# A hand-ordered attention-and-MLP kernel: the first loads cut into smaller pieces and moved between two DMA queues, and every step placed in a new order

## The chip, the cores and the metric

The kernel runs on one core of one Trainium2 chip. The core has five engines that run their own instruction streams: PE (TensorE, matrix products; its weight loads are listed apart as PEld), DVE (VectorE), ACT (ScalarE), POOL (GpSimd) and SP (SyncE, which here only issues DMA transfers). DMA transfers are issued from two queues: SP's, and ACT's, where the issuing instruction stands between ACT's arithmetic. The metric is device microseconds of one execution, lower is better.

## The reference

One normalised input feeds two branches, and the results are added to the input (2048 tokens of 448 features, 16 heads of 28, 1792 hidden features):

```
xn = layernorm(x)
q, k, v = split(xn @ wqkv)                       # 16 heads of 28
pq, pk = q @ w_phi, k @ w_phi                    # per head
phi = concat(softmax(p), softmax(-p))            # for q and for k
kv  = phi_k^T v ;  z = sum over tokens of phi_k
A   = (phi_q kv / (phi_q z + 1e-6)) @ wo
h   = xn @ w1 + b1 ;  act = h * tanh(softplus(h))   # "mish"
out = x + A + act @ w2
```

The matrix `w_phi` is folded into the query and key weights in the kernel: `Wpq = Wq w_phi` and `Wpk = Wk w_phi` are computed once, on PE.

## The kernel before

The 2048 tokens are 16 tiles of 128 (t = 0 to 15), taken in 8 pairs u. 448 features are three chunks of 128 rows and a tail of 64; a product over a chunk of 64 rows uses one half of PE's rows, so two products of a pair of tiles run side by side (the profile's rows of form `64*128`), and each pair's product is cut into the parts A, B (six matmuls each) and H (two, for the tail).

Nothing is scheduled by a compiler. A table of names, `ORDER` (line 147), lists about 600 steps; each step is a small function that appends instructions to the engines' streams, and every engine executes its own stream strictly in the order of the table. Waits between engines are derived from the data. PSUM has 8 banks, used as four pairs; a step takes the pair that was used least recently at that place in the table (`take2`, line 421), so the table also decides which earlier read must be over before a product may start.

The names that matter here (a digit is the tile, the pair or the chunk; a letter at the end is the engine: a ACT, d DVE, p POOL, s SP's queue, b both ACT and DVE, m DMA):

- `lxA.B` loads x tiles A to B-1; `lkm`, `lkt` load the main rows and the tail rows of Wk (`lkt` brings the tail of Wk and Wv for one half of the rows, 64x896), `lvm`, `lvt` the main rows of Wv and the other tail (64x448); `lqT0-3` load Wq transposed, a DMA transpose each (`load_qT`, L307); `lp` loads w_phi in 4 transfers, `lb` b1; `l1c0-2`, `l1t` W1 by chunks of rows and its tail, `l2p0-3` W2 in four parts, `lo` Wo.
- `st` statistics of a tile, `rt`/`rs` its 1/std, `xn` the normalised tile, `xt` its transpose (by PE and a read-out, or by DMA when it ends in m).
- `wtk0`, `wtk1` transpose the two halves of Wk on PE (L583); `wmk`, `wmq` compute Wpk and Wpq (L613). `wtk1` needs the tail that `lkt` brings.
- `v`, `k`, `q` are the three projections of a pair (L464); the read-out of k and q is two exponentials on ACT (L720, L793), that of v a copy on ACT or DVE (L544, L546).
- `kn`, `kc` turn the exponentials of k into softmax values: a sum and a reciprocal on DVE (L728 to L741), two multiplications on POOL (L732, L744). `kn` does one sign, `kc` both.
- `kv` (L761) sums phi_k^T v over all pairs; `kvz` reads it out; `e` transposes the q exponentials by DMA (L801); `nd` (L834) computes numerator and denominator of a tile; `ot` transposes the result by DMA; `wo` (L956) multiplies by Wo.
- `f0.n`, `f1.n` are the first MLP product of 128 hidden features over half of the tokens (L464) with mish on ACT (L814); `g` (L939) is the second; `sto`, `stt` store pairs and tiles.
- `z`, `y` are products of zeros on PE (L405) that touch no result. `qd` (L311) copies the last 64 columns of the transposed Wq, and `wmq` waits for it. `pw`, `pp`, `pv`, `pk`, `pi` set constants on POOL.

The program has three stages. In the front the loads arrive, the first four tiles are normalised and Wpk and Wpq are made. In the second stage PE runs the projections, with ACT's exponentials and POOL's multiplications behind it, up to `kv`. The last stage is the MLP and the attention output, with little else than PE's products.

Of the kernel before, what the change touches and what calls it, by code (L numbers as in the profile page):

```python
# [144 lines left out]


ORDER = """
zero pw pp table lx0.2a lkma lx2.4s lkta lvta lbs st2d st1d lx4.6a pi st3a z11 st0d lps rt1a lvms rt3a rt2p xn1a xn2d
rt0p xn3d lx10.12s b1 xn0d wtk0b wtk1b xt1a lx8.10a xt0d lqT3 wmk0a st4d lqT2 st5d wmk1a v1Ba rt4p lqT1 xn4p lqT0 v0Ba
l1c0a v1Aa lx6.8s lx12.14s l1c1s v0Ha st10d v1Ha rt5p qd v0Aa st11d k1A k1H wmq1a st9d rt10p rt9p wmq0a rt11p k0B k1B  # L150
xn5d st8d k0A rt8p st7d xn10d q0A st12d xn11d xn8p xt2m k0H st6d st13d q0H xn9d q1B lx14.16s rs3p xn7d q0B xn6d q1A
rt12p st15d rt13p k2A xn12d xt5m k2H xn13d v2Ad q1H k2B q2B st14d xt4m v2Bd q2A k5A xt3m v2Hd rs7p xt6m q2H xn15p k5B
v5Ba k5H v4Aa v5Ha v4Ha xn14a kn2.0 k4H kn0.0 kc5 kn2.1 k4A v4Ba v5Aa k4B e2 k3B e3 xt7m v6Hd l1c2s v6Ad k3H q4H k3A
l1ts v6Bd e0 q4B kn0.1 k6B kn4.1 kn4.0 q4A pv k6H v7Bd k7H k6A k7B v7Hd los f0.8B v7Ad ep k7A f0.8H f0.6B f0.4B e5
f0.6A f0.8A f0.6H v3Ba f0.4A e8 v3Ha f0.7B v3Aa f0.1A kn1.0 f0.4H f0.7A f0.7H kc6 kn7.1 e1 f0.1H kn7.0 f0.3B f0.1B q7B
f0.3H kn1.1 f0.3A q5H kn3.1 e4 q3B q5B q3H e9 q3A q5A f1.4B kn3.0 q7H q7A f1.4A l2p1s kv0 kv7 e11 kv4 kv6 kv5 pk kv2
kv3 kv1 e14 f1.12B kvz f1.3B e10 f1.12A f1.4H wob f1.3A f1.3H f0.12B f1.12H f1.9A f1.9H f0.5H f0.5A f1.9B f0.0H f0.5B
f0.0B nd1 f0.0A f0.9A e15 f0.12H f0.9H f0.12A nd0 f0.10A e6 f0.9B f1.10B f0.10H f1.6A f1.6H nd2 l2p0a f0.10B f1.6B
l2p3s ot0m f1.10A f1.10H f1.1H f1.11B f1.1A f1.11H nd4 f1.1B f1.7B f1.11A e7 f1.8H nd3 f1.7A f1.8B f1.0H f1.0A ot1m
f1.7H f0.13H f0.13A f1.0B f1.5H f0.13B f1.8A f1.5B nd6 f0.2B f1.5A f0.2H f1.2H f0.2A f1.2A nd5 f1.13H f1.2B f1.13B  # L160
f0.11A l2p2a f0.11H nd7 q6A f1.13A q6H f0.11B ot2m q6B wo0H ot3m wo0A nd11 nd10 wo0B e12 g1 g7 e13 ot5m g0 wo3A nd12
nd13 wo2A wo2H wo3B ot6m wo2B nd14 wo3H g6 g5 g11 g4 g10 nd15 wo5B wo6A ot7m nd9 wo5A sto2 wo5H nd8 wo6B g12 g2 g8 g3
g14 ot4m wo1H wo4B wo1B wo7B wo4A wo1A wo6H wo4H wo7H wo7A sto0 g13 g9 sto1 stt14 g15 sto6 sto5 y0.1 sto3 sto4 y3.4
stt15
"""


# [942 lines left out]
```

## Time and profile before

| what | us |
|---|---|
| median of 3 runs | 155.65 |
| the three runs | 150.18, 155.79, 155.65 |
| the profiled execution's own time | 150.82 |
| its span (first to last instruction) | 149.0 |
| busy in the span: PE, DVE, ACT, POOL | 145.1, 99.3, 76.3, 43.2 |

The span is 1.82 us shorter than the time of the same execution. PE's busy time counts a matmul until its modelled end, so neighbours overlap; how fast PE really goes is read from the starts. The granted TensorE clock is 1.00 in the whole profiled execution.

```profile
PE   7897999999999999999999999999999999999996
DVE  0885999999999303089794799588993399301722
ACT  3895999998988995774757839400000000000000
POOL 5425683999999992000000000000000000000000
DMA  4999459999997038974702133943030023220252
```

Each digit is a fortieth of the span, 3.7 us, in tenths. ACT and POOL end at about half of the span, DMA is full in the first 45 us, and PE has digits under 9 in the first four slices and in the last.

### The profile page before, as it was taken

The page shows a single profiled execution, that of the slowest core. Times are in us where ns is not written, and L with a number is a line of the kernel's source. Part 1 is how long each engine was busy: PE and PEld are TensorE (multiplying, and loading weights), DVE is VectorE, ACT ScalarE, POOL GpSimd, SP SyncE. Part 2 cuts the span into 40 slices and gives each one's busy share as a digit, 9 for nine tenths or more (in the row PEclk, how much of TensorE's full clock was granted, in tenths as well). Part 3 has the DMA queues.
Part 4 walks back from the last instruction along what each step waited for, and adds up shares of the span by engine and source line. Part 5 has one row for each costly group of instructions (what it writes and reads, how often), then busy time and mean ns, then how long its engine had stood idle before and what let it go on. Part 6 is the DMA issues. An engine that isn't in the chain of part 4 may idle for free.

```text
span 149.0 us, 3632 instructions
## 1 busy us (share of the span) xinstructions
PE 145.1 (97%) x1544; PEld 75.2 (50%) x1545; DVE 99.3 (67%) x222; ACT 76.3 (51%) x91; POOL 43.2 (29%) x66
## 2 busy tenths in 40 slices
PE   7897999999999999999999999999999999999996
PEld 2464544555444484454444545545555555547453
DVE  0885999999999303089794799588993399301722
ACT  3895999998988995774757839400000000000000
POOL 5425683999999992000000000000000000000000
DMA  4999459999997038974702133943030023220252
GB/s 121 320 249 317 106 132 164 157 239 218 212 224 183 4 57 107 191 168 122 133 4 40 26 92 66 109 93 62 7 62 0 0 41 87 56 67 4 92 185 92
DMA packets 40372, 17.17 MB, mean 115 GB/s; under 512 B 34084, under 2 KB 39844, under 8 KB 40356
## 3 DMA queue, kind: packets, MB, share of 16 engines
q1 hardware_dynamic: 38148, 14.37, 48.4%
q10 hardware_dynamic: 2208, 2.56, 5.8%
q8 instruction: 12, 0.20, 0.6%
q14 instruction: 4, 0.03, 0.1%
HBM read 6.97 MB, written 1.84 MB: 59 GB/s over the span
## 4 chain that ended last, share of the span: by engine, by line
PE 90%; SPq 5%; DMA 3%; issue 0%; DVE 0%
PE PS L464 48%; PE PS L939 28%; PE PS L956 7%; DMA WqT<-in_A_wqkv_dram 3%; SPq L307 2%; PE PS L834 2%; PE PS L761 2%; SPq L330 1%; PE PS L405 1%; PE PS L613 1%; SPq L287 1%; SPq L334 0%; SPq L290 0%; PE PS L921 0%; DVE WqT L311 0%
## 5 line engine op out<-in xcount | busy, mean ns | idle before, releaser
L464 PE MATMUL PS<-xnT,W 64*128 64x512 bf16 x392 | 45.3, 376 | 0.0
L939 PE MATMUL PS<-W,actT 128*128 128x448 bf16 (+1 forms) x224 | 42.7, 351 | 0.0
L814 ACT ACTIVATE actT<-PS,b1T 128x1024 bf16<-128x1024 f32 x28 | 30.1, 1112 | 12.2 <-PE PS L464 12.2
L939 PEld LDWEIGHTS PS<-W,actT 128*128 128x128 bf16 x224 | 21.6, 98 | 20.7 <-issue 1.3
L464 PEld LDWEIGHTS PS<-xnT,W 64*128 64x128 bf16 x392 | 18.1, 94 | 21.3 <-ACT actT L814 0.8
L904 DVE TENSOR_TENSOR x_all<-PS,x_all 128x448 bf16<-128x448 f32 (+1 forms) x16 | 9.3, 615 | 17.0 <-PE PS L956 9.2
L732 POOL TENSOR_TENSOR actT<-actT,rSk 128x896 bf16<-128x896 bf16 x12 | 20.0, 1697 | 0.0
L720 ACT ACTIVATE actT<-PS 128x896 bf16<-128x896 f32 x16 | 14.2, 1034 | 0.7 <-PE PS L464 0.7
L464 PE MATMUL PS<-Wpk,xnT 64*128 64x448 bf16 x112 | 13.2, 349 | 0.0
L464 PE MATMUL PS<-Wkv,xnT 64*128 64x448 bf16 x112 | 13.1, 349 | 0.1
L464 PE MATMUL PS<-Wpq,xnT 64*128 64x448 bf16 x112 | 13.0, 349 | 0.0
L728 DVE TENSOR_REDUCE Sk<-actT 128x32 f32<-128x896 bf16 x12 | 12.5, 1040 | 0.0
L849 DVE COPY Sq<-PS 128x16 f32<-128x16 f32 x32 | 4.0, 168 | 12.1 <-PE PS L834 12.1
L501 DVE BATCH_NORM_STATS2 stats<-x_all 128x6 f32<-128x448 bf16 x15 | 9.2, 610 | 4.1 <-DMA x_all<-in_A_x_dram 4.1
L860 DVE TENSOR_TENSOR xn<-v_all,rden 128x448 bf16<-128x448 f32 x16 | 10.0, 624 | 2.2 <-DMA Wkv<-xn 1.7
L857 DVE TENSOR_TENSOR v_all<-v_all 128x464 f32<-128x464 f32 x16 | 10.3, 643 | 0.6
L853 DVE TENSOR_TENSOR v_all<-PS,Sq 128x464 f32<-128x464 f32 x16 | 10.3, 641 | 0.5
L855 DVE TENSOR_TENSOR v_all<-PS,Sq 128x464 f32<-128x464 f32 x16 | 10.1, 630 | 0.0
L793 ACT ACTIVATE actT<-PS 128x896 bf16<-128x896 f32 x10 | 8.8, 987 | 0.3 <-PE PS L464 0.3
L464 PEld LDWEIGHTS PS<-Wkv,xnT 64*128 64x128 bf16 x112 | 5.3, 94 | 5.5 <-ACT actT L720 0.3
L464 PEld LDWEIGHTS PS<-Wpq,xnT 64*128 64x128 bf16 x112 | 5.3, 94 | 5.3 <-ACT Eq L793 0.3
L464 PEld LDWEIGHTS PS<-Wpk,xnT 64*128 64x128 bf16 x112 | 5.4, 94 | 5.1 <-ACT actT L793 0.4
(84 smaller groups left out, 135.5 us busy)
## 6 DMA issues: line engine op xcount, KB each, us to landing
out_dram<-x_all SPq DMA_DIRECT2D x7, 224.0 KB, 2.2
W<-in_B_w_dram SPq DMA_DIRECT2D x3, 448.0 KB, 4.9
x_all<-in_A_x_dram SPq DMA_DIRECT2D x5, 224.0 KB, 4.4
W<-in_B_w_dram ACTq DMA_DIRECT2D x2, 448.0 KB, 3.8
x_all<-in_A_x_dram ACTq DMA_DIRECT2D x3, 224.0 KB, 3.8
Wo<-in_A_wo_dram SPq DMA_DIRECT2D x2, 336.0 KB, 5.3
W<-in_B_w_dram SPq DMA_DIRECT2D x2, 224.0 KB, 4.9
Wkv<-in_A_wqkv_dram ACTq DMA_DIRECT2D x1, 336.0 KB, 4.4
```

What stands on the lines that cost most here:

```text
L464: ins = e.matmul(o, lhs(c, k), rhs(c, k), start=first and n == at[par][0], stop=last and n == at[par][-1])
L720: op("ACT", lambda e, s=s: e.activation(E_of(u)[:, s, :, :], two(b, D), ACT.Exp, scale=1.0 if s == 0 else -1.0), r=[pb(b), pb(b + 1)], w=[ ...
L728: op("DVE", lambda e: e.tensor_reduce(Sk[u][:, s, :], Eh(), AX.X, ALU.add), r=[("E", u, s)], w=[("Sk", u, s)], tag=f"Sk{u}.{s}")
L732: op("POOL", lambda e: e.tensor_tensor(Eh(), Eh(), ap_on(rSk[u][:, s, 0:1], [[1, 2 * H], [0, DH]]), ALU.mult), r=[("E", u, s), ("rSk", u, ...
L814: op("ACT", lambda e: e.activation(actT[:, q, fc, :], bank(b, 2), ACT.Mish, bias=b1T[:, fc:fc + 1]), r=[("b1T",), pb(b), pb(b + 1)], w=[(" ...
L853: op("DVE", lambda e: e.tensor_tensor(tv(t1[i]), num(0), sx(1), ALU.mult), r=[pb(b), pb(b + 1), ("Sq", i, 1)], w=[("t1", i)], tag=f"ta{t}")
L855: op("DVE", lambda e: e.tensor_tensor(tv(t2), num(1), sx(0), ALU.mult), r=[pb(b), pb(b + 1), ("Sq", i, 0)], w=[("t2",)], tag=f"tb{t}")
L857: op("DVE", lambda e: e.tensor_tensor(t1[i], t1[i], t2, ALU.add), r=[("t1", i), ("t2",)], w=[("t1", i)], tag=f"tc{t}")
L860: op("DVE", lambda e: e.tensor_tensor(o_sb[(t // 2) % 2][:, t % 2, :].rearrange("p (h d) -> p h d", d=DH), t1[i][:, :, 0:DH], ap_on(rden[i ...
L904: op("DVE", lambda e: e.tensor_tensor(x_all[:, t, 0:n], bank(b)[:, 0:n], x_all[:, t, 0:n], ALU.add), r=[pb(b), ("x", t)], w=[("out", t)], ...
L939: ins = e.matmul(bank(b)[:, 0:width(t)], act_of(fc, t), W2[:, fc, 0:width(t)], start=first and fc == 0, stop=last and fc == FC - 1)
L956: ins = e.matmul(bank(b)[:, 0:w], oT_of(u)[lo:hi, cc * P:(cc + 1) * P], Wo[lo:hi, cc, 0:w], start=first and n == at[par][0], stop=last and ...
```

## The change

Only `ORDER` is different: not one function, tile or instruction form is new, but the same steps stand in another order, and some in another variant (another queue or engine). The first six lines of the table before and after:

```diff
-zero pw pp table lx0.2a lkma lx2.4s lkta lvta lbs st2d st1d lx4.6a pi st3a z11 st0d lps rt1a lvms rt3a rt2p xn1a xn2d
-rt0p xn3d lx10.12s b1 xn0d wtk0b wtk1b xt1a lx8.10a xt0d lqT3 wmk0a st4d lqT2 st5d wmk1a v1Ba rt4p lqT1 xn4p lqT0 v0Ba
-l1c0a v1Aa lx6.8s lx12.14s l1c1s v0Ha st10d v1Ha rt5p qd v0Aa st11d k1A k1H wmq1a st9d rt10p rt9p wmq0a rt11p k0B k1B
...
+lx1.2s zero lx2.4a lx0.1a st1d lbs table st2d lkms pw pi st3a lkta lps lx4.6s rt1p st0d xn1d rt2a z7 y2.4 lx8.12s lvma
+xn2d rt0a b1 lqT3 rt3p xn0d xn3d wtk0a lqT2 wtk1d lvta xt0b st5d xt1a st4d wmk0a lqT1 wmk1a v0Ba v1Aa st8d lqT0 v0Aa
+rt4a rt8p rt5p st11d st10d rs5p qd v1Ha lx6.8s v0Ha k1H st9d lx12.14s v1Ba xn5d lx14.16s l1ts k1B k0H xn4d wmq0a l2p3s
```

The x tiles 0 and 1 come one by one from two queues, tiles 8 to 11 in one transfer from SP's queue. `lkm` goes from ACT's queue to SP's, `lvm` the other way. On ACT's queue `lkt`, `lvm` and `lvt` now stand between ACT's first statistics and read-outs; the load of x tiles 8 and 9 and of W1's first piece, which stood behind them, are gone from there. W1's pieces come after the query weights: the tail first, chunk 0 on SP's queue behind the first DMA transpose of x, chunks 1 and 2 on ACT's queue between the exponentials. The line numbers of the changed kernel are one less, since the table is one line shorter.

ACT's stream from its start, before: all weight loads but Wv's main rows and Wq stand ahead of the arithmetic.

```order
L351 ACT_TABLE_LOAD
L287 DMA x_all<-in_A_x_dram 128x896
L290 DMA Wkv<-in_A_wqkv_dram 128x3x448
L304 DMA Wkv<-in_A_wqkv_dram 64x896
L304 DMA Wkv<-in_A_wqkv_dram 64x448
L287 DMA x_all<-in_A_x_dram 128x896
L493 ACTIVATE junk,mv<-x_all 128x448
```

ACT's stream from its start, after (`L492` to `L496` are the statistics of tile 3, `L512`, `L514` the 1/std of tiles 2 and 0, `Eq` and `xnT` the read-outs of `wtk0` and of the transposed x):

```order
L286 DMA x_all<-in_A_x_dram 128x896
L286 DMA x_all<-in_A_x_dram 128x448
L350 ACT_TABLE_LOAD
L492 ACTIVATE junk,mv<-x_all 128x448
L494 ACTIVATE rmean<-mv 128x1
L496 ACTIVATE junk,mv<-x_all,rmean 128x448
L303 DMA Wkv<-in_A_wqkv_dram 64x896
L512 ACTIVATE lnv<-mv,eps_col 128x1
L514 ACTIVATE rstd<-lnv 128x1
L289 DMA Wkv<-in_A_wqkv_dram 128x3x448
```

Three loads that stood at the head of the streams are now issued only when ACT has reached the statistics of tile 3 and the 1/std of tile 2; `wtk1` needs the first of them, and `L494` and `L496` wait for the results of the rows before them.

SP's stream up to the first transposes of x, before and after:

```order
L287 DMA x_all<-in_A_x_dram 128x896
L334 DMA b_rows<-in_B_b_dram 14x128
L330 DMA Wbd<-in_A_w_phi_dram 28x4x28 x4
L290 DMA Wkv<-in_A_wqkv_dram 128x3x448
L287 DMA x_all<-in_A_x_dram 128x896
L307 DMA_TRANSPOSE WqT<-in_A_wqkv_dram 128x448 x4
L287 DMA x_all<-in_A_x_dram 128x896 x2
L294 DMA W<-in_B_w_dram 128x1792
L551 DMA_TRANSPOSE xnT<-xn 128x7x128
```

After:

```order
L286 DMA x_all<-in_A_x_dram 128x448
L333 DMA b_rows<-in_B_b_dram 14x128
L289 DMA Wkv<-in_A_wqkv_dram 128x3x448
L329 DMA Wbd<-in_A_w_phi_dram 28x4x28 x4
L286 DMA x_all<-in_A_x_dram 128x896
L286 DMA x_all<-in_A_x_dram 128x1792
L306 DMA_TRANSPOSE WqT<-in_A_wqkv_dram 128x448 x4
L286 DMA x_all<-in_A_x_dram 128x896 x3
L297 DMA W<-in_B_w_dram 64x1792 x2
L339 DMA W<-in_B_w_dram 128x3x448
L550 DMA_TRANSPOSE xnT<-xn 128x7x128
```

One more issue stands ahead of the four transposes of Wq, and three x loads, W1's tail and a part of W2 stand between them and the first DMA transpose of x.

POOL's stream in the second stage, before (the multiplications of `kn` are L732, those of `kc` L744; `mask` and `KVT` are constants for `kvz`):

```order
L533 TENSOR_SCALAR xn<-x_all,rstd,shift 128x64
L533 TENSOR_SCALAR xn<-x_all,rstd,shift 128x384
L732 TENSOR_TENSOR actT<-actT,rSk 128x896 x2
L744 TENSOR_TENSOR actT<-actT,rSk 128x896 x2
L732 TENSOR_TENSOR actT<-actT,rSk 128x896 x4
L371 MEMSET v_all 128x256
L732 TENSOR_TENSOR actT<-actT,rSk 128x896
L744 TENSOR_TENSOR actT<-actT,rSk 128x896 x2
L732 TENSOR_TENSOR actT<-actT,rSk 128x896 x5
L380 MEMSET mask 128x56
```

After:

```order
L388 MEMSET KVT 128x512
L507 TENSOR_SCALAR lnv<-mv 128x2
L509 TENSOR_TENSOR rstd<-lnv,mhalf 128x2
L507 TENSOR_SCALAR lnv<-mv 128x2
L509 TENSOR_TENSOR rstd<-lnv,mhalf 128x2
L731 TENSOR_TENSOR actT<-actT,rSk 128x896
L532 TENSOR_SCALAR xn<-x_all,rstd,shift 128x448
L743 TENSOR_TENSOR actT<-actT,rSk 128x896 x2
L731 TENSOR_TENSOR actT<-actT,rSk 128x896 x2
L743 TENSOR_TENSOR actT<-actT,rSk 128x896 x10
L731 TENSOR_TENSOR actT<-actT,rSk 128x896
```

There are 16 multiplications in both, but now 6 pairs belong to a `kc`, which can begin only when both signs of a pair of tiles are there; the constants stand ahead of them, and the last multiplication of all, `kn4.0`, belongs to the pair that `kv` takes last but one (`kv4`, after `kv0 kv2 kv7 kv1 kv3 kv6`).

PE's own stream has the same products. Ahead of the first `wmq` stand 38 matmuls of v and k instead of 36. The copies of v6 and v7 go to ACT (DVE before), those of v2 and v5 to DVE (v2, v6 and v7 before), so ACT has six of them instead of five, four of them behind Wpq instead of three; the normalised tile that ACT makes in the second stage is 15 instead of 14, and tile 1 is normalised on DVE instead of ACT. At the end, the two groups of zero products `y0.1` and `y3.4` behind the last product are gone: the 11 zero products ahead of the front stay, written as `z7` and `y2.4`.

More of the change, by code (lines that the diff above doesn't have):

```diff
@@ L147 @@
 ORDER = """
-zero pw pp table lx0.2a lkma lx2.4s lkta lvta lbs st2d st1d lx4.6a pi st3a z11 st0d lps rt1a lvms rt3a rt2p xn1a xn2d
-rt0p xn3d lx10.12s b1 xn0d wtk0b wtk1b xt1a lx8.10a xt0d lqT3 wmk0a st4d lqT2 st5d wmk1a v1Ba rt4p lqT1 xn4p lqT0 v0Ba
-l1c0a v1Aa lx6.8s lx12.14s l1c1s v0Ha st10d v1Ha rt5p qd v0Aa st11d k1A k1H wmq1a st9d rt10p rt9p wmq0a rt11p k0B k1B
-xn5d st8d k0A rt8p st7d xn10d q0A st12d xn11d xn8p xt2m k0H st6d st13d q0H xn9d q1B lx14.16s rs3p xn7d q0B xn6d q1A
-rt12p st15d rt13p k2A xn12d xt5m k2H xn13d v2Ad q1H k2B q2B st14d xt4m v2Bd q2A k5A xt3m v2Hd rs7p xt6m q2H xn15p k5B
@@ L153 @@
[L153 to L162, printed above, removed]
@@ L163 @@
-g14 ot4m wo1H wo4B wo1B wo7B wo4A wo1A wo6H wo4H wo7H wo7A sto0 g13 g9 sto1 stt14 g15 sto6 sto5 y0.1 sto3 sto4 y3.4
-stt15
+lx1.2s zero lx2.4a lx0.1a st1d lbs table st2d lkms pw pi st3a lkta lps lx4.6s rt1p st0d xn1d rt2a z7 y2.4 lx8.12s lvma
+xn2d rt0a b1 lqT3 rt3p xn0d xn3d wtk0a lqT2 wtk1d lvta xt0b st5d xt1a st4d wmk0a lqT1 wmk1a v0Ba v1Aa st8d lqT0 v0Aa
+rt4a rt8p rt5p st11d st10d rs5p qd v1Ha lx6.8s v0Ha k1H st9d lx12.14s v1Ba xn5d lx14.16s l1ts k1B k0H xn4d wmq0a l2p3s
+xt2m rt9p wmq1a pv k0A xn11d k1A st12d pp l1c1a k0B q1A xn10p st6d q0A q0H q1B q0B st7d q1H rs3p v2Bd k2B st13d l1c0s
@@ new lines @@
+xt5m ep xn8d xn9d v2Ad k2H xn6d st15d xn7d v2Hd pk rs6p q2B xt4m xn13d st14d rs7p k2A xt3m q2A xn12d q2H v5Ad k5B v5Bd
+k5H k4B kn1.1 xn15a xt6m v5Hd k5A k4H v4Ha k4A v3Ha xn14p l1c2a v4Aa e3 v3Ba k3B kc2 v3Aa xt7m v4Ba e1 k6B k3A k3H
+v6Ha k6H kn4.1 k6A e2 k7A k7H v6Aa k7B q4B kn1.0 e5 kc3 v6Ba q4H v7Ba q4A v7Aa f0.7B f0.8B f0.7H kc5 v7Ha e0 kc7 f0.8H
+f0.6H f0.8A f0.6B f0.3B e9 f0.6A f0.7A f0.3A kc0 f0.3H f0.4A q7B f0.4H f0.1B f0.4B f0.1H f0.1A e8 q3H q7A q7H q5H e4
+q3A q5B kc6 q3B f1.4A q5A f1.4B kv0 kn4.0 l2p2s kv2 kv7 kv1 kv3 kv6 e14 e10 kv4 kv5 f1.12B kvz f1.4H f1.9A f1.12A
@@ new lines @@
+f1.9H f1.12H f1.8B f1.9B e11 f1.7H f1.7A f1.8H f1.8A f0.12H f1.7B e7 nd3 f0.12A f0.5A e15 f0.12B f0.5H f1.3H f0.9H
+f0.5B f0.9A f1.3A nd1 f0.9B f1.10H f1.3B f1.10A l2p0s l2p1s f1.0B f1.10B nd0 f1.13B ot0m f1.0A f0.2H f1.13H f1.0H
+f1.13A f0.10B f0.2B nd4 f0.10H f0.2A f0.10A f0.0B nd5 f1.6B f0.0H e6 los f1.5B f1.6A f1.6H f0.0A f1.5A nd2 f1.1A f1.1H
+f1.5H ot1m f1.11H f1.1B f1.11A f0.11H f0.13B f1.11B nd6 f0.11B f0.13H f0.13A f1.2A f0.11A f1.2B nd7 wo0B ot3m q6B
+f1.2H wo0A q6A q6H ot2m wo0H nd11 nd10 g1 g5 g4 e13 g0 wo3H nd13 wo2B e12 wo3A nd12 ot5m wo3B wo2A wo2H nd15 g7 ot6m
@@ L165 @@
+g11 g6 wo5H nd8 wo6A wo5A wo6B nd9 nd14 wo5B g10 ot4m wob g9 g13 sto5 ot7m g8 g12 g14 wo7H wo6H sto2 wo1B wo4A wo1A
+wo7B wo4H wo1H wo7A stt14 wo4B g3 g2 sto3 sto1 g15 sto0 sto4 sto6 stt15
 """
```

## The prediction

> **What bounds the kernel now.** I read the chain that ended last first, then the windows by stage, then PE's and the queues' timelines in the front. The chain (start, length, what):
>
> ```profile
> 8.56 5.07 DMA WqT<-in_A_wqkv_dram
> ...
> 13.65 0.24 DVE WqT L311
> ...
> 13.94 0.96 PE PS L613 x16
> 14.90 37.59 PE PS L464 x382
> 52.49 3.27 PE PS L761 x128
> 55.75 7.88 PE PS L464 x72
> ...
> 146.11 0.41 PE PS L921 x14
> ```
>
> Up to 13.94 us the end hangs on the last transpose of Wq, issued at 8.56; from there to 146.52 only PE's own order is on the chain. Busy time by window (PE, PEld, DVE, ACT, POOL, clock):
>
> ```profile
> 14.90:52.40 37.50, 37.50 (x382) 18.14 (x382) 33.65 (x66) 35.42 (x43) 32.30 (x33) 1.00 0.87 163
> 52.40:146.50 94.10, 94.10 (x1050) 49.94 (x1050) 56.92 (x130) 30.70 (x30) 4.08 (x10) 1.00 0.36 77
> ```
>
> PE has no idle time behind 14.90, at a granted clock of 1.00. The same products must run after the change, so nothing can be won there, only lost: ACT has 2.1 us of slack in the 37.5, POOL 5.2. What can be won is the front:
>
> ```profile
> 0.96 4.68 PE L405 MATMUL PS<-zeros 128*128 128x512 bf16 x11 [0.96 <-POOL zeros L357]
> ...
> 5.71 1.31 PE L583 MATMUL PS<-ident,Wkv 128*112 128x128 bf16 x16
> 7.43 1.22 PE L539 MATMUL PS<-ident,xn 128*128 128x128 bf16 x14 [0.42 <-DVE xn L527]
> 8.49 0.95 PE L613 MATMUL PS<-Wbd,Eq 112*128 112x112 bf16 x16
> 9.51 2.82 PE L464 MATMUL PS<-Wkv,xnT 64*128 64x448 bf16 x28
> 12.16 0.92 PE L464 MATMUL PS<-Wpk,xnT 64*128 64x448 bf16 x8
> ```
>
> Start to start, 28 matmuls of the form 64x448 take 12.16 - 9.51 = 2.65 us, 0.095 us each; so the 36 ahead of the query weights end at 9.51 + 36 x 0.095 = 12.9, and PE waits 1.0 us to 13.94. With 0.4 us ahead of L539 and some tenths between the others that makes about 2 us of gaps in the front: more than 2 us (1.3%) this change can hardly win.
>
> **The sum is made against** the profiled execution, 150.82 us (span 149.0 and 1.8 around it). The runs read 150.18, 155.79 and 155.65: the profiled execution is at their lower end, 3.1% under the median. No row explains the other 5 us, since the rows are of one execution. A change under about 2% can't be told from none in this kernel.
>
> **Part 1, the front.** The issues on SP's queue now:
>
> ```profile
> 4.19 0.48 SPq L287 DMA_DIRECT2D x_all<-in_A_x_dram  x1
> 4.71 5.12 SPq L307 DMA_TRANSPOSE WqT<-in_A_wqkv_dram  x4
> ```
>
> One more x load stands ahead of the transposes: they start 0.5 later, at 5.2, the last is issued at 9.1. How long they take to land depends on what else moves. Of the list of DMA issues (how many, KB each, us to landing): two rows of its window 8.0 to 9.8 us, two of the first 20 us, and the bounds of all x loads (L287):
>
> ```profile
> W<-in_B_w_dram ACTq DMA_DIRECT2D x1, 448.0 KB, 4.2
> x_all<-in_A_x_dram ACTq DMA_DIRECT2D x1, 224.0 KB, 3.8
> ...
> Wkv<-in_A_wqkv_dram ACTq DMA_DIRECT2D x1, 112.0 KB, 4.4
> ...
> xnT<-xn SPq DMA_TRANSPOSE x2, 2.9
> ...
> DMA to landing us min/median/max: 2.7/3.9/5.0
> ```
>
> An uncrowded transpose lands 2.9 us after its issue, this one took 5.07: the last Wq lands between 12.0 and 14.2. The first two rows, 672 KB on ACT's queue, travelled beside it; now 392 KB of Wv do, and earlier. I take the middle, 13.0.
>
> [...]
>
> But PE must reach `wmq` first. The tail of Wk, which `wtk1` needs, was issued early in ACT's queue; now it stands behind ACT's statistics of tile 3:
>
> ```profile
> 4.13 0.58 ACT L493 ACTIVATE junk<-x_all 128x448 bf16<-128x448 bf16 x1 [2.03 <-DMA x_all<-in_A_x_dram]
> ...
> 5.07 0.67 ACT L497 ACTIVATE junk<-x_all,rmean 128x448 bf16<-128x448 bf16 x1
> ...
> 7.87 0.75 DVE L546 COPY Eq<-PS 112x512 bf16<-112x512 bf16 x2
> ```
>
> Tile 3 lands as before (first in ACT's queue, a transfer of the same size on each), so the load is issued when L497 goes out, at 5.1, and lands by the bounds of the x loads at 7.8 to 10.1. I take 3.0 us, 8.1, near the lower end: the piece is half of an x pair and its queue is empty. PE in order: `wtk0` to 6.35 (half of 1.31), idle to 8.1, `wtk1` to 8.75, the 14 transposes of x 0.8 (the 1.22 less its gap of 0.4), `wmk` 0.95: v starts at 10.5 instead of 9.51. That covers the later Wv, issued about 6.1 behind L497 and a 1/std: at the median of 3.9 it lands at 10.0. With 38 matmuls (3.6) `wmq` starts at 14.1. DVE comes out there too: the read-out of `wtk1` to 9.7, half a transpose to 10.1 (0.4, half of 0.75), five statistics of 0.75 (rows below) to 13.85, then `qd`, 0.24, to 14.1. Wq at 13.0 is no longer last. Against 13.94 that is +0.2, and two more matmuls are done (-0.2): **0.0**. Ends: -1.0 if the tail lands as soon as PE wants it (v at 9.5, `wmq` at 13.1, less 0.2), +1.9 if it takes 5.0.
>
> **Part 2, POOL ahead of `kv`.** The rows of the softmax of k:
>
> ```profile
> 18.80 0.62 DVE L501 BATCH_NORM_STATS2 stats<-x_all 128x6 f32<-128x448 bf16 x1
> ...
> 19.55 0.59 DVE L501 BATCH_NORM_STATS2 stats<-x_all 128x6 f32<-128x448 bf16 x1
> ...
> 22.47 0.88 DVE L527 TENSOR_SCALAR xn<-x_all,mv,rstd 128x448 bf16<-128x448 bf16 x3
> ...
> 23.26 0.62 DVE L501 BATCH_NORM_STATS2 stats<-x_all 128x6 f32<-128x448 bf16 x1
> ...
> 24.01 1.07 DVE L546 CAST v_all<-PS 128x896 bf16<-128x896 f32 x1
> ...
> 25.39 1.08 DVE L728 TENSOR_REDUCE Sk<-actT 128x32 f32<-128x896 bf16 x1
> ...
> 26.50 0.35 DVE L730 RECIPROCAL rSk<-Sk 128x32 f32<-128x32 f32 x1
> ...
> 28.11 1.96 DVE L738 TENSOR_REDUCE Sk<-actT 128x64 f32<-128x1792 bf16 x1
> ...
> 30.10 0.56 DVE L741 RECIPROCAL rSk<-Sk 128x64 f32<-128x64 f32 x1
> ...
> 30.74 3.35 POOL L744 TENSOR_TENSOR actT<-actT,rSk 128x896 bf16<-128x896 bf16 x2 [0.23 <-DVE rSk L741]
> ...
> 38.21 0.86 DVE L397 SCALAR_TENSOR_TENSOR epsT<-epsT 128x1 f32<-128x1 f32 x1
> ...
> 46.31 8.32 POOL L732 TENSOR_TENSOR actT<-actT,rSk 128x896 bf16<-128x896 bf16 x5
> ```
>
> POOL's last multiplication ends at 54.63 before; `kv`, 3.27 / 8 = 0.41 us a pair from 52.49, gets there without a wait. Now DVE works from `qd` (14.1) through seven statistics of 0.75 (5.25), nine tiles of xn (five in two pieces and four whole; one of each takes 23.26 - 22.47 = 0.79, so 3.6), `ep` and three shifts (0.86 and some tenths, 1.3), two copies of v (2.1), `kn1.1` (1.4) and the sums of `kc2` (2.5): 16.15, to 30.25. From there POOL has 15 multiplications of 1.67, 25.05: to 55.3. PE reaches `kv4`, the seventh, at 52.49 + 6 x 0.41 = 54.95. With the hand-over that is **+0.4**; ends 0 (DVE a little quicker) and +1.4 (DVE a microsecond later).
>
> **Part 3, ACT in the second stage.** Two more copies of v stand between Wpq and the first mish:
>
> ```profile
> 28.06 1.91 ACT L544 ACTIVATE v_all<-PS 128x896 bf16<-128x896 f32 x2
> ...
> 39.26 1.28 ACT L814 ACT_TABLE_LOAD   x1
> ```
>
> Two take 1.91, so ACT changes its table at 41.2 instead of 39.26. PE has 242 matmuls of v, k and q behind `wmq` (14.1 + 0.96 + 242 x 0.095 = 38.05) and fills the time with `f0.7` and `f0.8`; `f0.6`, 16 matmuls of 0.109 later, at 39.8, takes q4's banks, which ACT frees a copy ahead of its table, at 40.2. A stall of 0.4 there only makes PE later at `kv4` and eats the wait of part 2, so the larger of the two counts and nothing is added; ends 0 and +1.0, should ACT come later.
>
> **At nothing:** the zero products behind the end lay beside the last stores. W1's last chunk goes out between ACT's exponentials of k4, about 30, and at 4.2 us lands at 34, ahead of `f0` at 38; past 8 us it would stall PE. The constants on POOL come earlier and only free `kvz`. The stores at the end stand closer together but go out before the last one is due; 0 to +0.4 if they hold it up.
>
> Sum: 0.0 + 0.4 = +0.4, **151.2 us**.
>
> **Rivals.** (1) The front is won whole: the tail of Wk lands at once, Wq at 12.0, DVE keeps up, POOL is not late: -1.0, so 149.8. For it: 0.4 MB less ahead of Wq. Against: the tail's issue at 5.1 is fixed by ACT's rows. (2) Slower: the tail of Wk holds PE, since `wtk1` stands ahead of all else in PE's order. At 5.0 us to land it is +1.9 and 152.7; over 2% it gets only from 6.2 us to landing, at 11.3 (+3.1, 153.9). For it: the 4.4 of the same piece before. Against: that one stood behind an x pair and Wk's main rows. (3) The second stage gives way: ACT's copies or POOL's `kv4` stall PE by 1.3 more than I sum, 152.5; ACT is the engine with least slack there. (4) The change doesn't do what it says: three loads stay in ACT's queue inside the front, and the front, now bound by them, stays as long as before: 150.8. [...] The 11 products of zeros run at 0.43 us each, twice what 512 columns take later (55.75 to 63.63: 72 matmuls, two side by side, 0.22 a pair); if PE's wait from 6.3 to 8.1 set the clock back, the 38 + 16 matmuls behind it would take some 4.5 us more: 155.3. Against: behind its own wait of 1.0, at 13.94, the trace goes on at full pace (37.59 us for 382 matmuls from 14.90 on). [...] (6) The reading: the runs of one and the same program lie 5.6 us apart, so the changed one may be read at its upper end, about 155.8.
>
> **Chances.** My sum and (4) 0.51, (1) 0.13, (2) 0.10 of which 0.03 over 2%, (3) 0.09 of which 0.02 over, (5) 0.02, (6) 0.15. The likeliest cases alone span 149.6 to 152.8, which is (1) to the ends of (2) and (3); the range is **149.4 to 155.9**, since (6) is too likely to leave out. Faster by over 2%: 0.12, which is a part of the first two cases, where the lower reading stands against the median of 155.65. Slower: 0.03 + 0.02 + 0.02 + 0.03 (of 6) = 0.10. Within: 0.78.
>
> **What would show it.** L582's second half starts near 8.1 (right) or by 7 or past 9 (wrong); L463's first v matmul near 10.5; L612 with WqT near 14; a wait ahead of L760's last 32 matmuls of some tenths on POOL; no other PE gap behind. A PE gap inside 15 to 50, or one of over half a microsecond behind `kv`, would make the sum wrong, and so would v starting by 9.5.

## The result

The changed kernel takes 155.08 us, the median of six runs (154.26 to 156.21); the kernel before took 154.03 (150.18 to 155.79). The comparison leaves out runs more than 1.5% above the fastest of the same kernel, which of the kernel before keeps those from 150.18 to 150.77; against these the changed kernel takes 1.0309 times as long, 95% interval 1.0222 to 1.0395. It is **slower**, and none of its six runs comes near 151.2. The profiled execution is one of 154.58 us (span 152.8), 3.76 more than the profiled execution before (150.82, span 149.0).

The chain of work that ended last, of the changed kernel (start us, us, what; its line numbers are one less than those before):

```profile
4.76 0.01 ACT junk L496
4.77 5.08 DMA Wkv<-in_A_wqkv_dram
...
9.89 0.94 PE PS L582 x8
10.83 1.61 PE PS L538 x14
12.44 1.40 PE PS L612 x16
13.85 3.70 PE PS L463 x38
17.55 0.89 PE PS L612 x16
18.44 37.52 PE PS L463 x380
55.96 3.45 PE PS L760 x128
```

The chain no longer runs through Wq. It goes through ACT's statistics of tile 3, through the load issued behind them (the tail of Wk, 5.08 us to landing, at 9.85), and through `wtk1`, which PE could start only then. From 13.85 on it is PE's order alone. PE's timeline in the front (start, length, line, what, how many) shows the wait, in brackets with what ended it, and what it did to the products behind it:

```profile
5.88 1.07 PE L582 MATMUL PS<-ident,Wkv 128*112 128x128 bf16 x8
9.89 0.94 PE L582 MATMUL PS<-ident,Wkv 128*112 128x128 bf16 x8 [2.94 <-DMA Wkv<-in_A_wqkv_dram]
10.77 1.68 PE L538 MATMUL PS<-ident,xn 128*128 128x128 bf16 x14
12.23 1.61 PE L612 MATMUL PS<-Wbd,Eq 112*128 112x112 bf16 x16
13.78 2.25 PE L463 MATMUL PS<-Wkv,xnT 64*128 64x448 bf16 x22
...
17.48 0.71 PE L612 MATMUL PS<-Wbd,WqT 112*128 112x112 bf16 x11
```

The 16 products with phi (L612) take 1.61 us where they took 0.95 before, without a gap. The windows show why (from and to, length, busy time of PE, PEld, DVE, ACT and POOL, the granted clock, then the DMA engines' busy share and GB/s):

```profile
6.85:10.20 3.35, 0.41 (x6) 0.29 (x4) 0.79 (x3) 1.02 (x1) 0.00 (x0) 1.00 1.08 233
10.20:13.55 3.35, 3.35 (x36) 3.23 (x34) 2.50 (x7) 1.56 (x3) 0.00 (x0) 0.50 1.19 274
...
18.40:150.20 131.80, 131.79 (x1429) 70.45 (x1428) 86.08 (x179) 67.30 (x74) 33.76 (x36) 1.00 0.48 96
```

After a stretch in which PE was busy for 0.41 us of 3.35, TensorE runs at half its clock: the trace has 0.50 from 10.20 to 13.61, 3.41 us. Behind 18.4 us PE is busy without a gap at full clock, as before.

So the 3.8 us are found in one place. The query weights start at 17.48 instead of 13.94, 3.54 later, and two more matmuls are done by then (0.19): 3.35. `kv` takes 3.45 instead of 3.27 (0.18), and 0.3 are spread over the rest. Against the forecast, v starts 13.78 - 10.5 = 3.28 later: 1.8 from the tail's landing (`wtk1` at 9.89 instead of 8.1), 1.5 from the clock.

The mean granted clock of this execution is 0.989, as in the run of 154.26. In the other four runs of the changed kernel, 154.97 to 156.21, it is 0.978. One stretch of 3.41 us at half clock takes 1.7 / 152.8 = 0.011 off the mean, so by an estimate from these numbers they spent about one more at half clock; no trace shows where.

### The profile page after: what moved, and what is told of

Read it like the earlier page. It is cut to its first block, busy times and chain, and to the rows that moved or that the text cites. A ratio compares the mean times of both kernels' runs of the same rounds, so it can differ in the third digit from the quotient of the medians.

```text
span 152.8 us, 3611 instructions
## 1 busy us (share of the span) xinstructions
PE 146.3 (96%) x1540; PEld 79.2 (52%) x1540; DVE 97.5 (64%) x214; ACT 77.6 (51%) x93; POOL 40.5 (27%) x58
## 4 chain that ended last, share of the span: by engine, by line
PE 91%; DMA 5%; ACT 1%; DVE 0%; issue 0%
PE PS L463 49%; PE PS L938 28%; PE PS L955 7%; DMA Wkv<-in_A_wqkv_dram 3%; PE PS L833 2%; PE PS L760 2%; DMA x_all<-in_A_x_dram 2%; PE PS L612 2%; PE PS L538 1%; PE PS L582 1%; ACT junk L492 0%; DVE x_all L903 0%; ACT rmean L494 0%; DVE x_all L924 0%; ACT junk L496 0%
## 5 line engine op out<-in xcount | busy, mean ns | idle before, releaser
L463 PE MATMUL PS<-xnT,W 64*128 64x512 bf16 x392 | 44.7, 376 | 0.0
L463 PEld LDWEIGHTS PS<-xnT,W 64*128 64x128 bf16 x392 | 19.1, 94 | 20.5 <-ACT actT L813 0.3
L463 PE MATMUL PS<-Wkv,xnT 64*128 64x448 bf16 x112 | 13.6, 349 | 0.0
L463 PE MATMUL PS<-Wpq,xnT 64*128 64x448 bf16 x112 | 12.5, 349 | 0.0
L737 DVE TENSOR_REDUCE Sk<-actT 128x64 f32<-128x1792 bf16 x6 | 11.9, 1979 | 0.8 <-ACT actT L719 0.8
L463 PEld LDWEIGHTS PS<-Wpq,xnT 64*128 64x128 bf16 x112 | 5.9, 94 | 5.0 <-ACT Eq L792 0.3
L463 PEld LDWEIGHTS PS<-Wkv,xnT 64*128 64x128 bf16 x112 | 5.8, 94 | 4.7 <-ACT actT L792 0.4
L463 PEld LDWEIGHTS PS<-Wpk,xnT 64*128 64x128 bf16 x112 | 5.9, 94 | 4.5 <-ACT actT L719 0.2
```

The source lines that it names most:

```text
L463: ins = e.matmul(o, lhs(c, k), rhs(c, k), start=first and n == at[par][0], stop=last and n == at[par][-1])
L737: op("DVE", lambda e: e.tensor_reduce(Sk[u][:, :, :].rearrange("p s n -> p (s n)"), E_of(u).rearrange("p s i (h f) -> p (s i h) f", f=DH), ...
```

## The experiments

Each kernel was timed beside the kernel before on one chip; ratios are formed as above, against that kernel's runs there. Of the table of names only the parts with moved names are shown; other lines are left out. "Front theory" is the reading above: the late tail, and the clock that its wait sets back. Where a run missed the time that was expected ahead of it, that is said.

**One part of the change alone, in the kernel before.** Only the tail of Wk is issued later; everything else is the kernel before.

```diff
-lx0.2a lkma lx2.4s lkta lvta lbs st2d st1d lx4.6a pi st3a
+lx0.2a lkma lx2.4s lvta lbs st2d st1d lx4.6a pi st3a lkta
```

> The kernel before with one part of the change alone: the tail of Wk issued behind ACT's statistics of tile 3 instead of at 1.78 us. Front theory: it is issued at 5.1 and, behind the main rows of Wv, two x pairs and beside the transposes of Wq, lands at 9 to 10 instead of 6.2; PE waits 2.6 to 3.7 us from 6.35, v starts at 12 to 14, the query weights at 15.7 to 17.6: 152.6 to 154.6 us where Wq comes in time, and a clock of 0.989 in most runs. Rival (in the old order the tail has cover: PE's wait of 1.0 us for Wq takes it up, and one load alone is worth no more than that): at most 151.8 us in its quick runs.

154.63 us (five runs, 153.35 to 154.99), ratio 1.0307 (1.0287 to 1.0327): one issue costs as much as the whole change, 1.0309. The profiled execution is the shortest of the five, 153.35; its clock is 0.989, that of the other four 0.978. Its chain:

```profile
5.01 4.06 DMA Wkv<-in_A_wqkv_dram
...
9.11 0.75 PE PS L583 x8
...
16.64 0.89 PE PS L613 x16
17.53 37.59 PE PS L464 x382
```

The tail lands at 9.07, PE waits 2.2 us, and the clock falls again (0.50 in the window from 10.20 to 13.55, 1.70 us for the 16 products with phi on PE's timeline). The front theory's numbers hold in this execution but for the wait, which it put at 2.6 or more.

**The wait against the clock.** Nine products of zeros in PE's wait; they change no result, and the tail is issued as late as before.

```diff
-xn2d rt0a b1 lqT3 rt3p xn0d xn3d wtk0a lqT2 wtk1d
+xn2d rt0a b1 lqT3 rt3p xn0d xn3d wtk0a z9 lqT2 wtk1d
```

> The changed kernel with nine products of zeros (128 x 512, as those at the start) put in PE's order between the two halves of the transposes of Wk: they add no work that is wanted and fill PE's wait for the tail (2.0 us of it at full pace, 3.9 at half). Clock theory (of the loss of 3.5 us, 1.5 are the half clock from 10.2 to 13.55): the tail lands near 9.85 as before, the granted clock stays 1.00 behind it, the 14 transposes of x take 0.8 and the 16 products 0.8 us, and v starts at 12.2 to 12.6: 152.9 to 153.4 us in the profile, and the clock of all runs higher than 0.978 to 0.989. Rival (all 3.5 us are the wait, and the clock costs nothing): v starts at 13.8 and the time stays 154.5.

152.90 us (152.56 to 154.69), ratio 1.0104 (0.9969 to 1.0239); 152.56 in the profiled execution, 2.0 below that of the changed kernel and under the 152.9 to 153.4 expected. PE's timeline, and the window that had been idle with the one behind it:

```profile
6.57 2.13 PE L404 MATMUL PS<-zeros 128*128 128x512 bf16 x9
9.49 0.75 PE L582 MATMUL PS<-ident,Wkv 128*112 128x128 bf16 x8 [0.80 <-DMA Wkv<-in_A_wqkv_dram]
10.18 0.96 PE L538 MATMUL PS<-ident,xn 128*128 128x128 bf16 x14
10.97 0.95 PE L612 MATMUL PS<-Wbd,Eq 112*128 112x112 bf16 x16
11.85 2.25 PE L463 MATMUL PS<-Wkv,xnT 64*128 64x448 bf16 x22
```

```profile
6.85:10.20 3.35, 2.55 (x18) 1.23 (x17) 0.88 (x3) 0.94 (x1) 0.00 (x0) 1.00 1.03 197
10.20:13.55 3.35, 3.35 (x49) 2.45 (x50) 3.17 (x10) 2.77 (x4) 0.00 (x0) 1.00 1.18 296
```

Useless work made the kernel faster. From the start of `wtk1` to the first v it takes 11.85 - 9.49 = 2.36 us instead of 13.78 - 9.89 = 3.89: the clock cost 1.5 us. The other 0.4 of the 2.0 is the tail, which came 0.4 earlier in this execution. The products of zeros didn't keep the clock up every time: the longest of the four runs, 154.69, has 0.989, the other three 0.999 and 1.000.

**What makes the tail late.** The 448 KB of x tiles 8 to 11 move behind three transposes of Wq on SP's queue.

```diff
-lkta lps lx4.6s rt1p st0d xn1d rt2a z7 y2.4 lx8.12s
+lkta lps lx4.6s rt1p st0d xn1d rt2a z7 y2.4
...
-lqT1
+lqT1 lx8.12s
```

> The changed kernel with the 448 KB load of x tiles 8 to 11 moved in SP's queue behind three transposes of Wq; the tail of Wk is issued at 4.8 as before. Front theory (the tail's 5.08 us are the 672 KB of x that were issued shortly ahead of it on the other queue): only the pair 4 and 5 stands ahead, which landed at 8.32, so the tail lands at 8.2 to 8.8, PE waits 1.3 to 1.9 us, v starts at 10.7 to 12.0: 151.6 to 153 us. Rival (it is slow because of its own shape or queue, 64 rows of 1792 bytes): it lands near 9.8 again, 154.5 us.

Of the list of DMA issues (KB each, us to landing), the same load in the changed kernel, then in this one:

```profile
Wkv<-in_A_wqkv_dram ACTq DMA_DIRECT2D x1, 112.0 KB, 5.1
```

```profile
Wkv<-in_A_wqkv_dram ACTq DMA_DIRECT2D x1, 112.0 KB, 3.3
```

The tail lands at 8.31, so it was held by the bytes issued ahead of it on the other queue (with the 448 KB ahead it took 5.08 us in the changed kernel and 4.6 and 5.9 in the variants with products of zeros and with `wtk1` behind). Yet 154.33 us (152.97 to 154.64), ratio 1.0273 (1.0224 to 1.0322): behind a wait of 1.7 us the clock fell here too (to 0.50, rows in the last section), v starts only at 12.27 (10.7 to 12.0 expected), and the 151.6 to 153 expected hold for the profiled execution alone (152.97).

**Undoing the late tail in the changed kernel.**

```diff
-lx1.2s zero lx2.4a lx0.1a st1d lbs table st2d lkms pw pi st3a lkta
+lx1.2s zero lx2.4a lx0.1a lkta st1d lbs table st2d lkms pw pi st3a
```

> The changed kernel with one issue moved back: the tail of Wk at the head of ACT's queue, behind tile 0, ahead of the table load and ACT's statistics. Front theory (the loss is the late tail of Wk and the clock that its wait sets back): no PE wait ahead of the second half of the transposes of Wk, which start near 6.9 instead of 9.89; granted clock 1.00 behind 7 us; v starts at 9.5 to 10.2, the query weights at 13.4 to 14.2; 150.2 to 151.3 us, 3.5 to 4 less than the changed kernel's profile. Later-order theory (the new order behind the front, or POOL ahead of kv, costs it): the front is mended but 153 us or more remain, with a PE gap behind 20 us.

152.51 us (152.07 to 152.82), ratio 1.0053 (0.9956 to 1.0149): 2.6 us won in the medians, 1.8 in the profiled executions, not the 3.5 to 4 expected. PE's timeline, and the load issued by ACT at 5.75:

```profile
6.67 2.04 PE L582 MATMUL PS<-ident,Wkv 128*112 128x128 bf16 x16 [0.72 <-DMA Wkv<-in_A_wqkv_dram]
...
12.10 2.26 PE L463 MATMUL PS<-Wkv,xnT 64*128 64x448 bf16 x22 [0.90 <-DVE stats L500]
```

```profile
Wkv<-in_A_wqkv_dram ACTq DMA_DIRECT2D x1, 336.0 KB, 6.2
```

The row names DVE, but the product also needs Wv, whose main rows landed at 5.75 + 6.22 = 11.97: the second load that the change put behind ACT's statistics was hidden by the first. By the rows PE was slow here too, up to about 10 us, though the trace has the clock at 1.00: the 16 transposes of Wk (L582) take 8.64 - 6.67 = 1.97 us from start to start. In the last variant of the changed kernel below (W1 and W2 one load at a time) they take 1.13. The wait for Wv covers that loss.

**All three loads ahead of ACT's statistics**, `lkta` as above, `lvma` and `lvta` ahead of `st3a`:

```diff
-lx1.2s zero lx2.4a lx0.1a st1d lbs table st2d lkms pw pi st3a lkta lps lx4.6s rt1p st0d xn1d rt2a z7 y2.4 lx8.12s lvma
+lx1.2s zero lx2.4a lx0.1a lkta st1d lbs table st2d lkms pw pi lvma lvta st3a lps lx4.6s rt1p st0d xn1d rt2a z7 y2.4 lx8.12s
...
-wtk1d lvta
+wtk1d
```

> The changed kernel with all three loads that ScalarE issues late (tail of Wk, main rows and tail of Wv) moved ahead of ACT's statistics of tile 3; the rest of the new order stays. In the run with the tail alone moved, Wv (issued at 5.75, landed at 11.97) held v until 12.10. Front theory: Wv lands by 9.5, v starts at 9.7 to 10.5, the query weights at 13.8 to 14.4 (Wq again lands near 13.4 and DVE doubles it then); clock 1.00 throughout; POOL makes PE wait 0.2 to 0.6 us at kv; 150.7 to 151.8 us. Later-order theory: v as early as this, yet 152.5 us or more.

153.00 us (152.75 to 153.97), ratio 1.0214 (1.0180 to 1.0248), not the 150.7 to 151.8 expected. With Wv issued early too, Wk's main rows take 5.67 us to landing instead of 4.0 and are there at 7.41 instead of 5.80, PE waits for them, and the clock is at half from 7.43 to 10.84:

```profile
7.46 2.04 PE L582 MATMUL PS<-ident,Wkv 128*112 128x128 bf16 x16 [2.35 <-DMA Wkv<-in_A_wqkv_dram]
```

**PE's order instead of the load's.** `wtk1` behind the transposes of x and the first product with phi:

```diff
-wtk0a lqT2 wtk1d lvta xt0b st5d xt1a st4d wmk0a
+wtk0a lqT2 lvta xt0b st5d xt1a st4d wmk0a wtk1d
```

> The changed kernel with the second half of the transposes of Wk moved in PE's order behind the transposes of x and the first product with phi, which do not need the tail. Front theory: the tail still lands near 9.85, but 14 + 8 matmuls (about 1.3 us at full pace) run in the wait; PE's idle time is cut from 2.9 to about 1.7 us (in two pieces, since xn must be there), v starts at 12 to 12.6 instead of 13.78 if the clock keeps full, and at 13.0 to 13.4 if it falls to half all the same; 152.0 to 153.8 us. Later-order theory: 154.5 us, as v's start decides nothing.

154.26 us (152.49 to 155.27), ratio 1.0131 (0.9966 to 1.0296): inconclusive, and above the 152.0 to 153.8 us expected. In the profiled execution, the longest of its runs, the tail landed at 10.71 and PE waited 2.0 us for it and 0.8 for the read-out; the clock fell all the same, from 12.63 to 16.05.

**From the query weights to the end.** In all these kernels the time from the start of `wmq` to the end of the span is nearly the same, so the front decides (the starts are those on PE's timelines):

| kernel | v starts | wmq starts | span | wmq to end |
|---|---|---|---|---|
| before | 9.51 | 13.94 | 149.0 | 135.1 |
| before, tail late | 12.56 | 16.57 | 151.6 | 135.0 |
| changed | 13.78 | 17.48 | 152.8 | 135.3 |
| changed, products of zeros | 11.85 | 15.55 | 150.8 | 135.2 |
| changed, x behind | 12.27 | 15.97 | 151.2 | 135.2 |
| changed, `wtk1` behind | 13.16 | 18.27 | 153.5 | 135.2 |
| changed, tail first | 12.10 | 15.80 | 151.1 | 135.3 |
| changed, three loads first | 11.76 | 15.46 | 151.2 | 135.7 |

**Does the new order cost by itself?** Two kernels mend the front further. One takes over the front loads of the kernel before:

```diff
-lx1.2s zero lx2.4a lx0.1a st1d lbs table st2d lkms pw pi st3a lkta lps lx4.6s
+zero pw table lx0.2a lkma lx2.4s lkta lvta lbs st2d st1d lx4.6a pi st3a lps lvms lx10.12s
...
-lx8.12s lvma
...
-lvta
...
-xt1a
+xt1a lx8.10a
```

> The changed kernel's order of all steps behind the front, with the loads of the front as the kernel before issues them (Wk whole and Wv's tail by 2.4 us on ACT's queue, Wv's main rows and one x pair ahead of Wq on SP's, x tiles 8 and 9 on ACT's), but W1 later as in the change. Front theory: Wk is there by 6.3, no PE wait of over 1 us, v starts at 9.4 to 10; with no W1 beside it Wq lands at 12 to 13.5 and the query weights start at 13.2 to 14.1; from their start to the end of the span the changed kernel and its variants took 135.2 to 135.4 us: 150.1 to 151.3 us, level with the kernel before. Later-order theory: a front as before, and 152 us or more.

153.46 us (152.83 to 154.28), ratio 1.0224 (1.0173 to 1.0276), not the 150.1 to 151.3 expected. Here DVE's statistics, in the new order, wait for tiles 8 and 9 ahead of `qd`, and then the transposed x of pair 2 is late (PE's waits for these two: in all, times, longest):

```profile
PE PS L463 <- DMA xnT<-xn: 1.4, 1, 1.4
PE PS L612 <- DVE WqT L310: 1.2, 1, 1.2
```

The other puts both tails at the head of ACT's queue and Wv's main rows on SP's, ahead of x tiles 4 and 5 (`lvms`):

```diff
-lx0.1a st1d lbs table st2d lkms pw pi st3a lkta lps lx4.6s
+lx0.1a lkta lvta st1d lbs table st2d lkms pw pi st3a lps lvms lx4.6s
...
-lx8.12s lvma
+lx8.12s
...
-wtk1d lvta
+wtk1d
```

> The changed kernel with the tails of Wk and Wv at the head of ACT's queue and Wv's main rows on SP's queue ahead of x tiles 4 and 5 (with all three on ACT's queue the main rows of Wk landed at 7.41 and PE waited 2.3 us for them). If it is the bytes ahead that set a landing: Wk's main rows land at 6.3 to 6.8, the tail before them, PE waits under 1 us and its clock stays, v starts at 9.6 to 10.8 and the query weights at 14 to 14.8, as Wq comes 0.5 later: 151 to 152 us. Rival: Wk's main rows land past 7 again, PE waits about 2 us, the clock falls, 152.8 us.

The front is better than that of the kernel before: v at 9.48, the query weights at 13.38. The time is the worst so far, 157.29 us (153.77 to 158.53), where 151 to 152 were expected. In the profiled execution, its longest, PE waits 5.8 us for the transposed x of pair 2, a step on the chain:

```profile
14.88 9.57 DMA xnT<-xn
```

W1's tail, W2's last part and W1's chunk 1, over 1.2 MB, had been issued between 12.3 and 15.7. In the changed kernel this transpose, issued at 17.61, landed at 20.87, and nobody waited, because PE itself was 3.5 us late. The next three kernels keep this front and move those loads (their diffs are against the one just shown). Behind the transpose of pair 2 they make the next pair late:

```diff
-l1ts k1B k0H xn4d wmq0a l2p3s xt2m
+k1B k0H xn4d wmq0a xt2m l1ts l2p3s
...
-pp l1c1a
+pp
...
-k2B
+k2B l1c1a
```

> The changed kernel with its front mended (tails of Wk and Wv first in ACT's queue, Wv's main rows on SP's queue ahead of x tiles 4 and 5), and now also W1's tail, W2's last part and W1's chunk 1 behind the transposed x of pair 2, which in the run without this landed at 24.46 and held PE for 5.8 us. Theory: the query weights start at 13.2 to 14.0, the transposed x lands by 19.5 and PE waits at most 0.8 us for it; with 135.3 us from the query weights to the end of the span, and 0.2 to 0.6 for POOL at kv: 150.3 to 151.8 us, 3 to 4 under the changed kernel. Rival (the order behind the front costs by itself): 152.5 us or more with no wait for the transposed x.

158.07 us (155.91 to 160.71), ratio 1.0513 (1.0474 to 1.0553), where 150.3 to 151.8 were expected: pair 2 was in time, pair 5 took 7.47 us and held PE for 3.9. With the loads of SP's queue behind three or four transposes, and chunk 1 on ACT's later still:

```diff
-l1ts k1B k0H xn4d wmq0a l2p3s xt2m
+k1B k0H xn4d wmq0a xt2m
...
-pp l1c1a
+pp
...
-st13d l1c0s
+st13d
...
-xt4m
+xt4m l1ts l1c0s
...
-xt3m
+xt3m l2p3s
...
-k5B
+k5B l1c1a
```

> The changed kernel with its front mended as in the two runs before (Wv on SP's queue, both tails first on ACT's), and the loads of W1 and W2 behind the first three transposed x pairs (2, 5, 4) on SP's queue, W1's chunk 1 later on ACT's, so that none stands ahead of a transpose that PE is about to need. Theory (the order behind the front costs only through transfers that arrive late): transposed x of pair 2 lands by 17.8, of pair 5, issued at 19.0 behind DVE's tiles, by 22.5, PE needs it at 22.8; PE waits under 0.5 us in all, and 150.3 to 151.5 us come out. Rival (DVE and POOL of the new order cost by themselves): a wait of PE for POOL at kv of 1 us or more, or 152.5 us and above with no late transfer.

158.20 us (155.60 to 158.97), ratio 1.0308 (1.0204 to 1.0412), where 150.3 to 151.5 were expected: three loads now stood ahead of pair 3, 9.82 us to landing, and PE waited 5.5. One load at a time (the removals as in the diff above):

```diff
-xt4m
+xt4m l1ts
...
-xt3m
+xt3m l1c0s
...
-l1c2a
+l1c1a l1c2a
...
-l2p2s
+l2p2s l2p3s
```

> The changed kernel with its front mended as before (Wv on SP's queue, both tails first on ACT's), and the loads of W1 and W2 one at a time: W1's tail behind the transposed x of pairs 2, 5 and 4, chunk 0 behind pair 3, chunks 1 and 2 on ACT's queue near 26 to 30 us, W2's last part much later. In the run before, three loads ahead of pair 3 made it land 9.8 us after its issue and held PE for 5.5 us. Theory (the order behind the front costs only through late transfers): pair 3 lands within 5.5 us of its issue at 22.5, PE waits at most 1 us in all behind 14 us, clock 1.00, 150.3 to 151.8 us. Rival (the order costs by itself): 152.5 us or more with no transfer over a microsecond late, or a wait for POOL at kv of 1 us or more.

151.52 us (151.25 to 152.89), ratio 1.0034 (0.9953 to 1.0115), inside the 150.3 to 151.8 expected. PE's waits behind 1 us (in all, times, longest):

```profile
PE PS L582 <- DMA Wkv<-in_A_wqkv_dram: 0.9, 1, 0.9
PE PS L463 <- DMA xnT<-xn: 0.5, 1, 0.5
PE PS L463 <- ACT actT L719: 0.3, 1, 0.3
```

With no transfer over half a microsecond late behind the front, the new order is as fast as the old one within the interval, 3.6 us under the changed kernel. A small cost of the order remains possible: its query weights start at 13.34, 0.6 ahead of the kernel before, yet its span is 149.8 instead of 149.0. From the query weights to the end it takes 136.5 us instead of 135.1. Of these 1.4 us, 0.8 are the last two waits, and 0.5 lie behind the start of `kv` (96.9 instead of 96.5 us).

**The second part of the change alone: W1 later.** In the kernel before, W1's first chunk leaves the front:

```diff
-l1c0a v1Aa lx6.8s
+v1Aa lx6.8s
...
-wmq0a
+wmq0a l1c0a
```

> The kernel before with the second part alone: W1's first 448 KB leave ACT's queue in the front (issue at 9.5) and go out behind the query weights' read-out. If W1 holds up the last transpose of Wq, this lands at 12.3 to 13.2 instead of 13.63, the query weights start 0.4 to 0.9 earlier (PE is ready at 12.9): 149.9 to 150.5 us beside 150.82 of the profile before. Rival (the last transpose is late because of x tiles 8 and 9, which land just ahead of it): it lands at 13.4 to 13.8 and the time does not move. W1 lands near 24, well before its use at 38, so no stall behind.

150.91 us, and all twelve runs lie between 150.65 and 151.26, while the kernel before ran from 149.72 to 156.75 beside them (median 153.51 of 18); ratio 1.0055 (1.0031 to 1.0079), where 149.9 to 150.5 us were expected. Wq's last transpose landed at 11.74, the query weights started at 12.89, 1.05 earlier, and PE gave 1.1 us back at 19.4, waiting for the transposed x of pair 2 that was issued behind W1's loads. With the chunk moved later still, and W1's next chunk behind that transpose (against the kernel before):

```diff
-l1c0a v1Aa lx6.8s lx12.14s l1c1s
+v1Aa lx6.8s lx12.14s
...
-xt2m
+xt2m l1c1s
...
-k2A
+k2A l1c0a
```

> The kernel before with W1's first 448 KB behind the first exponentials (about 19 us) and its second 448 KB behind the transposed x of pair 2 on SP's queue. With the first part alone the query weights started at 12.89 instead of 13.94, but the transposed x of pair 2, issued at 14.05 behind both loads of W1, landed at 19.29 and held PE for 1.1 us at 19.4. Theory (bytes ahead set the landing): it lands at 17 to 18.3, PE does not wait, span 148.0, 149.5 to 150.0 us in every run, about 1 us under the kernel with the first part alone. Rival (the transpose itself takes 5 us from its issue): it lands at 19 again and nothing is won: 150.7 to 151.0.

151.98 us (151.08 to 155.30), ratio 1.0109 (1.0059 to 1.0158), where 149.5 to 150.0 were expected: pair 2 was in time, pair 5 took 7.41 us and held PE for 2.4. With only the first chunk moved, to about 20 us (behind `q2A`):

```diff
-l1c0a v1Aa lx6.8s
+v1Aa lx6.8s
...
-q2A
+q2A l1c0a
```

> The kernel before with W1's first 448 KB issued at about 22 us on ACT's queue instead of 9.5 (13.9 in the run with that part alone, 18.1 in the one with two loads moved), and SP's queue as before. In the first of these runs the transposed x of pair 2 was 1.1 us late behind that load, in the second pair 5's 2.4 us late behind W1's other chunk. Theory: neither now has a fresh 448 KB ahead; both land within 4 us of their issue; the query weights start at 12.9 to 13.2 and PE waits under 0.3 us behind: 149.6 to 150.2 us in all runs, W1 there at 27, ahead of its use at 38. Rival (something else holds those transposes): PE waits 1 us near 19 again, 150.7 to 151.0.

PE's waits behind 1 us, in all, times and longest:

```profile
PE PS L464 <- DMA xnT<-xn: 0.3, 1, 0.3
PE PS L761 <- POOL actT L732: 0.2, 1, 0.2
```

150.48 us (twelve runs, 150.19 to 152.20; the kernel before beside them 152.80, 150.65 to 156.35), ratio 0.9925 (0.9882 to 0.9968): 0.75% less, which is inside the 2% that the prediction counts as no change, and 0.3 us above the 149.6 to 150.2 expected. It is the lowest median of all variants here, though on another chip the kernel before itself had a median of 149.97 (eight runs). What this version wins more clearly is the spread.

**The kernel before, as its own control.**

> The kernel before, unchanged, as its own control. [...] Rival (the transfers differ from run to run): long and short runs show the same clock.

The four runs, with their granted clocks: 150.90 (1.000), 153.60 (1.000), 155.41 (0.989) and 156.54 us (0.978). So both the clock and the transfers have a part: the two longest show a lower clock, but 153.60 is 2.7 us longer than 150.90 at the same clock. The profiled execution is the one of 155.41. Its chain and windows show another late load and the same fall of the clock:

```profile
8.56 8.11 DMA WqT<-in_A_wqkv_dram
...
16.98 0.96 PE PS L613 x16
```

```profile
14.65:18.00 3.35, 1.02 (x18) 0.92 (x20) 1.27 (x4) 0.42 (x1) 0.00 (x0) 1.00 0.82 274
18.00:21.35 3.35, 3.35 (x20) 1.39 (x18) 3.21 (x12) 2.56 (x6) 2.31 (x6) 0.50 0.38 77
```

The last transpose of Wq took 8.11 us in this execution, 5.07 in the one before, with the same loads ahead: 3 us of wait and 1.6 of clock (39.20 us for the 382 matmuls behind the query weights instead of 37.59). That accounts for the 4.6 us of this one execution; why the transfers took longer in it, the trace doesn't show. No run over 152.2 us is among the 24 with W1's first chunk alone moved, but one of 155.30 is among the six with two chunks moved; the other long executions left no trace, and their cause stays open.

## Why the prediction was wrong

**The landing of the tail of Wk failed, by size.** The step was "I take 3.0 us, 8.1, near the lower end: the piece is half of an x pair and its queue is empty". The issue came at 4.77 (5.1 forecast), the landing took 5.08 us, just past the upper bound of 5.0. That its own queue was empty counted for nothing; the 672 KB issued on the other queue at 4.03 and 4.45 did. Without the 448 of them it took 3.3.

The measured 155.08 lies inside the range of 149.4 to 155.9, but by luck: the upper end was put there for rival 6, the scatter of one and the same program, and no mechanism of the sum reaches so far. The 155.3 of rival 5, in which PE's wait sets the clock back, is as close by chance, since its price for the clock was three times too high and its landing of the tail 1.8 us too early.

**The clock failed, by its chance and its price.** Rival 5 had the right cause with a chance of 0.02, and put 4.5 us on it where 1.5 were lost, since only 3.41 us run at half pace, from 10.20 to 13.61. That PE's wait, 1.8 us in my sum, would be too short for it no run had shown; in the kernel with x behind the clock fell behind one of 1.7. It fell behind stretches of 3.35 us with 0.41, 1.02, 1.03, 1.19 and 1.40 us of PE's work (changed kernel, control, three loads first, tail late, x behind), and in the variant with `wtk1` behind, of 3.41 us with 1.03. The wait of 1.0 us ahead of 13.94 in the kernel before, which I took as evidence against, left 2.45 us of work in the 3.3 from 12.2 to 15.5, and the products of zeros left 2.55 in the 3.35 from 6.85; behind these two the clock stayed at 1.00.

**Rivals 2 and 5 were one case.** I priced the late tail at +1.9 with the clock at full, so that it passed 2% only at a landing of 6.2 us, and gave the clock a chance of its own. The wait that the first makes is the cause of the second: at 5 us to landing the two together are 1.8 + 1.5 = 3.3.

**The rest held.** Wq was no longer last: it landed at 13.05 (13.0 forecast), though DVE, itself behind PE, came to `qd` only at 15.8. PE has no gap behind 18 us. POOL held `kv` by at most 0.2 (+0.4 forecast): `kv` is 0.18 longer here, and in five variants PE's wait for POOL there is 0.2. ACT's two more copies stalled nothing at `f0`; in the mended kernel PE waited 0.3 for ACT, earlier, at 28.6. The removed zero products and the bunched stores together cost 0.2 at most (from PE's last wanted product to the span's end 2.6 instead of 2.4). Rival 1, the front won by a later W1, was right as a part: alone it brings the query weights 1.05 earlier, but the next transfer, the transposed x of pair 2, takes it back.
